# One Tanh of ScalarE moved behind copies in the projection, and one scaling on VectorE cut in two

## The chip, the cores and the metric

The kernel runs on one core of a Trainium2 chip. The metric is device time of one execution in microseconds (us); lower is better. A core has five engines that each work through their own list of instructions in order: TensorE (PE: matmul, with PEld for its weight loads), VectorE (DVE), ScalarE (ACT), GpSimd (POOL) and SyncE (SP, which here only issues transfers). They meet through semaphores: an instruction that needs another engine's result waits at the head of its engine's list, and all that is listed behind it waits too.

## The reference

`x` has 2048 tokens of 1024 features. It is normalised, and the normalised `xn` goes through two branches whose results are added to `x`:

```python
x = A_x
xn = _layernorm(x, axis=-1)
# branch A: a diagonal complex recurrence over the tokens
dt = jnp.exp(log_dt); Lam = Lambda_re + 1j * Lambda_im
Lam_bar = jnp.exp(dt * Lam)
B_bar = ((Lam_bar - 1.0) / Lam)[:, None] * Bmat
Bu = jnp.einsum("bld,pd->blp", x + 0j, B_bar)            # projection in (x is xn here)
h = Lam_bar[None, :] * h + Bu[:, t, :]                   # for every token t
y = 2.0 * jnp.einsum("blp,dp->bld", hseq, Cmat).real + x * Dskip
# branch B: a dense layer with mish
h = jnp.einsum("bsd,df->bsf", x, w1) + b1
sp = jnp.log1p(jnp.exp(-jnp.abs(h))) + jnp.where(h > 0, h, 0)
act = h * jnp.tanh(sp)
return jnp.einsum("bsf,fd->bsd", act, w2)
```

There are 1024 complex states, 3584 hidden features, and the output is bfloat16.

## The kernel before

The tokens are worked in four blocks of 512 (`blk` 0 to 3). A block has these stages, in the order in which TensorE goes through them:

1. First dense product (`first_tile`, line 777): 28 tiles `f` of 128 hidden features, 8 matmuls each, into PSUM bank `f % 8`. In blocks 1 to 3 ScalarE moves the first 7 tiles to `hb` with the bias (line 787), VectorE the others (line 790). Seven tiles are a group; when one is full, `mish` puts three activations on ScalarE over the whole group (128 x 3584): Exp (line 755), Ln of 1 + that (756), Tanh (757). `mish_mul` (762) is the product with `hb` on VectorE. Exp and Tanh need no table load between them, Ln needs one before it and Tanh one after it.
2. Projection into the states. Block 0 does it plainly (`project_in`). From block 1 on (`FAST = 1`) `project_fast` does it with seven products of half-size blocks in place of eight, for four pairs of state tiles a, b, c, d (`pr` 0 to 3). The order is the string `ORDER`: `c5` is product 5 of pair c (8 matmuls of 256 columns, line 834) and what takes its result away (`evacuate`); `r2` is the rotation of state tile 2 on VectorE (800 to 805); `u7` is a start on the second dense product for output unit 7 (6 matmuls, line 960); `m2` and `m3` are `mish_mul` of groups 2 and 3. A pair has three PSUM banks X, Y, Z; c has banks 4, 5, 6, and d has 0, 1, 2. Products 1, 6, 7 and 4 accumulate in X one after the other, and after products 1, 5 and 6 a copy of the partial sums is kept (a snapshot, `snaps`). Pairs a and b are copied by VectorE (849), pairs c and d by ScalarE (851): six copies a block. VectorE joins snapshots with other banks (859). The next product in bank X waits until the snapshot before it has been read out. There are four snapshot slots; a slot is free when its join has run. Product 4 goes from X to `hT` by a cast: on VectorE for a and b (876), on ScalarE for c and d (878).
3. Second dense product (`tail`, line 960, operands `ring` and `act`), then the recurrence's output projection (line 960, `ring` or in block 0 `CT`, and `hT`) into the same eight banks, one for each of the eight units of output. Meanwhile VectorE runs the rotations that are left, `mish_mul` of groups 2 and 3, the next block's normalisation and the recurrence (925 to 935).
4. `finish` (1027): VectorE adds banks and `x`, four times a block, two banks each. ScalarE issues the stores (1019).

Between block 0 and block 1 there is work that is done once: the rows of B and C are given scales by powers of two. `rows_C` writes a scaled C to DRAM (ScalarE, 1117, and its transfers, 1119). `scale_B(pr)` multiplies the two state tiles of a pair by a row, in two VectorE instructions, one for the real part (`ci` 0) and one for the imaginary part (`ci` 1), 128 x 2048 each (line 1126). `sums_B` (1137, 1138) then forms the sums that the seven products need. `scale_B(0)` is listed ahead of the four `finish` of block 0; `scale_B(1)` to `scale_B(3)` follow in `side(f)` of block 1, after tiles f = 0, 1 and 2. `rows_spread(1)` (1110) waits for a row that GpSimd's queue fetches (1103, 1105).

The lists are made in program order; nothing sorts them afterwards. So the place of a call is the place in its engine's list.

Of the kernel before, what the change touches and what calls it, by code (L numbers as in the profile page):

```python
# [163 lines left out]
def build_kernel(nc, A_x, A_Lambda_re, A_Lambda_im, A_B_re, A_B_im, A_C_re, A_C_im,  # L164
# [10 lines left out]
    NF = F // P  # L175
    GF = 7
# [4 lines left out]
    FAST = 1  # L181
# [7 lines left out]
    def sb(name, shape, dtype):  # L189
        return nc.alloc_sbuf_tensor(name, shape, dtype)  # L190
# [12 lines left out]
    act = sb("act", [P, NF, TB], bf16)  # L203
# [46 lines left out]
    def c(n):  # L250
        return cs[:, CN.index(n), :]
# [260 lines left out]
    def ln_skip(blk, q):  # L512

        i = blk % 2
        m = mt[:, q % 2, :, :].rearrange("p a t -> p (a t)")
        vop(lambda e: e.tensor_tensor(m, xn[:, q, :], dsk[:], op=ALU.mult),  # L516
            reads=[b_xn[q], b_dsk], writes=[b_m[q % 2]])
        vop(lambda e: e.tensor_tensor(xx[:, i, q, :], xx[:, i, q, :], m, op=ALU.add),
            reads=[b_xx[i][q], b_m[q % 2]], writes=[b_xx[i][q]])
# [7 lines left out]
    def b1(f):  # L527
        return par[:, 3 * NJ + f:3 * NJ + f + 1]
# [43 lines left out]
    def w1_tile(base, f, k):  # L572

        s = (base + 2 * (f // 4) + k // (NK // 2)) % NRING
        wt = ring[:, s, :].rearrange("p (k f) -> p k f", k=NK // 2)
        return s, wt[:, k % (NK // 2), (f % 4) * P:(f % 4 + 1) * P]
# [10 lines left out]
    def first_rest(f):  # L587

        for k in range(NK):
            s, w = w1_tile(0, f, k)  # L590
            PE.mm(lambda e, k=k, w=w: e.matmul(ps[:, f, 2 * P:4 * P], lhsT=w, rhs=xnT[:, k, 2 * P:4 * P],
                                               start=k == 0, stop=k == NK - 1),
                  reads=[b_ring[s]] + b_xnT[2:], writes=[b_ps[f]], first=k == 0, last=k == NK - 1)
# [155 lines left out]
               s_CT, writes=b_CT + b_early)  # L749


    def mish(g):
        hs = hb[:, (g % 2) * GF:(g % 2) * GF + GF, :]
        a = act[:, g * GF:(g + 1) * GF, :]
        aop(lambda e: e.activation(a, hs, AF.Exp), reads=[b_hb[g % 2]], writes=[b_act[g]])  # L755
        aop(lambda e: e.activation(a, a, AF.Ln, bias=1.0), reads=[b_act[g]], writes=[b_act[g]])  # L756
        aop(lambda e: e.activation(a, a, AF.Tanh), reads=[b_act[g]], writes=[b_act[g]])  # L757

    def mish_mul(g):
        hs = hb[:, (g % 2) * GF:(g % 2) * GF + GF, :]  # L760
        a = act[:, g * GF:(g + 1) * GF, :]
        vop(lambda e: e.tensor_tensor(a, a, hs, op=ALU.mult), reads=[b_act[g], b_hb[g % 2]], writes=[b_act[g]])  # L762
# [3 lines left out]
    def item_done():  # L766
        n_item[0] += 1
        ring_load()

    def first_tile(blk, f):  # L770
        bank, hs = f % 8, f % (2 * GF)
        raw = blk == 0 and f < NR
        if raw:
            first_rest(f)
        for k in range(0 if raw else NK):
            s, w = w1_tile(n_item[0], f % 4, k)
            PE.mm(lambda e, k=k, w=w: e.matmul(ps[:, bank, :], lhsT=w, rhs=xnT[:, k, :],  # L777
                                               start=k == 0, stop=k == NK - 1),
                  reads=[b_ring[s]] + b_xnT, writes=[b_ps[bank]], first=k == 0, last=k == NK - 1)
        if f % 4 == 3:  # L780
            item_done()
            item_done()
        if f % GF == 0 and f >= 2 * GF:
            mish_mul(f // GF - 2)
        ts = slice(2 * P if raw else 0, 4 * P)
        if blk and f < GF:
            aop(lambda e: e.activation(hb[:, hs, :], ps[:, bank, :], AF.Identity, bias=b1(f)),  # L787
                reads=[b_ps[bank], b_par], writes=[b_hbf[hs]])
        else:
            vop(lambda e: e.tensor_scalar(hb[:, hs, ts], ps[:, bank, ts], b1(f), None, op0=ALU.add),  # L790
                reads=[b_ps[bank], b_par], writes=[b_hbf[hs]])
        if f % GF == GF - 1:
            mish(f // GF)

    def banks_of(j):
        return 2 * ((j + 2) % 4)
# [41 lines left out]
    def evacuate(pr, n, keep):  # L838
# [34 lines left out]
        if n == 4:  # L873
# [3 lines left out]
            else:  # L877
                aop(lambda e: e.copy(dst, bank(X)), reads=[b_ps[X]], writes=b_hT[1][j0:j0 + 2])

    ORDER = ("a2 a1 b2 b1 a5 b5 a6 b6 a3 b3 a7 b7 c2 d2 a4 b4 c5 c1 r0 d5 d1 r1 c6 c3 d6 d3 "  # L880
             "c7 d7 u7 c4 r2 u5 d4 u6 u4 r3 r4 r5 r6 r7 m2 m3")

    def project_fast(open_unit):
        keep = {}
        for o in ORDER.split():
            kind, n = o[0], int(o[1])
            if kind == "r":
                rotate_in(n)
            elif kind == "u":
                open_unit(n)  # L890
            elif kind == "m":
                mish_mul(n)
            else:
                product("abcd".index(kind), n)
                evacuate("abcd".index(kind), n, keep)
# [213 lines left out]
    def rows_spread(h):  # L1109
        vop(lambda e: e.tensor_copy(srow[:, TB * h:TB * (h + 1)].rearrange("p (j q) -> p j q", q=P),  # L1110
                                    srow0[:, TB * h:TB * (h + 1)].rearrange("p (q j) -> p j q", q=P)),
            reads=[b_actf[26 + h]], writes=[b_actf[24 + h]])
# [5 lines left out]
            reads=[b_CT[j], b_si[j // 4]], writes=b_t)  # L1118
        AC.dma(lambda e: e.dma_start(ctd[j], t), s_ctd[j], reads=b_t, writes=[b_ctd[j]])

    def scale_B(pr):
        js = slice(2 * pr, 2 * pr + 2)
        b_B = b_BT[js]
        row = srow[:, 2 * P * pr:2 * P * (pr + 1)].rearrange("p (j q) -> p j q", j=2)
        for ci in range(2):
            vop(lambda e, ci=ci: e.tensor_tensor(  # L1126
                BT[:, ci, js, :, :], BT[:, ci, js, :, :], row.unsqueeze(2).to_broadcast([P, 2, NK, P]), op=ALU.mult),
                reads=b_B + [b_actf[24 + pr // 2]], writes=b_B)
# [25 lines left out]
    for blk in range(NB):  # L1154
        def side(f):
            if blk:
                if f in (8, 10, 12, 15):
                    ln_skip(blk, (8, 10, 12, 15).index(f))
                    if blk >= FAST:
                        sums_x((8, 10, 12, 15).index(f))  # L1160
                if blk == FAST:
                    if f == 1:
                        rows_spread(1)
                    if f < 3:
                        scale_B(f + 1)
                    if f in (3, 4, 17, 19):
                        sums_B((3, 4, 17, 19).index(f))
                return
            if f == 13:
                for j in range(NJ):  # L1170
                    table(j)
            if f in (5, 6, 7, 8):
                coefficients(f - 5)
            if f in (8, 9, 11, 12):
                ln_skip(0, (8, 9, 11, 12).index(f))
            if f in (14, 16, 18, 20):
                ln_stats_only(1, (f - 14) // 2)
            if f < 24 and f % 3 == 2:
                transpose_B(f // 3)
            if f >= 26:  # L1180
                transpose_C(f - 26)

        for f in range(NF):
            first_tile(blk, f)
            side(f)
        out_stage = tail(blk)
        open_unit = next(out_stage)
        if blk >= FAST:
            project_fast(open_unit)
        else:  # L1190
            project_in(blk)
        if 0 < blk < NB - 1:
            for q in range(NQ):
                ln_stats_only(blk + 1, q)
            ln_rsqrt()
            for q in range(NQ):
                ln_scale(blk + 1, q)
        if blk:
            next(out_stage)
        for j in range(NJ):  # L1200
            if blk == 0 and j == NJ - 1:
                rows_scale(0)
            recur(blk, j)
            if blk:
                continue
            if j == 0:
                mish_mul(3)
                ln_root()
                for q in range(NQ):
                    ln_scale(1, q)  # L1210
                next(out_stage)
                for i in range(NHS):
                    rows_load(i)
            scale_C(j)
            for i in {4: (0, 1, 2), 5: (3, 4, 5, 6), 6: (7, 8, 9, 10), 7: range(11, 16)}.get(j, ()):
                rows_size(i)
        if blk + 1 < NB:
            carry()
        if blk == FAST - 1:
            rows_scale(1)  # L1220
            vop(lambda e: e.tensor_tensor(qi[:], qi[:], c("ss").unsqueeze(1).to_broadcast([P, 2, NJ]), op=ALU.mult),
                reads=[b_qi] + b_ss, writes=[b_qi])
            rows_spread(0)
            scale_B(0)
            for j in range(NJ):
                rows_C(j)
        for _ in out_stage:
            pass
        if blk == FAST - 1:
            snaps_ready()  # L1230
# [36 lines left out]
```

## Time and profile before

| what | us |
|---|---|
| median of three runs | 615.79 (615.63 to 615.86) |
| the profiled execution's own time | 614.92 |
| its span, first to last instruction | 613.7 |
| TensorE busy in the span | 607.1 |
| VectorE busy | 491.1 |
| ScalarE busy | 306.5 |
| GpSimd busy | 95.3 |

The span is what the trace shows; 1.2 us of the execution's own time lie around it. The mean clock that was granted to TensorE is 1.000. The stages of the four blocks are found in the trace by their line numbers: the first dense product of block 1 begins at 162.02 us, of block 2 at 313.82 us. In the timeline's rows, a matmul group's length takes in the time until its last result is written, so a group that follows without a gap begins about 0.17 us before the end of the one ahead of it.

### The profile page before, as it was taken

How to read it: one execution, taken by the hardware profiler on the slowest of the kernel's cores; microseconds unless marked ns; L12 is line 12 of the kernel's file. 1: busy time of each engine (PE TensorE's matmuls, PEld its weight loads, DVE VectorE, ACT ScalarE, POOL GpSimd, SP SyncE). 2: the span in 40 equal slices, each digit the busy share in tenths (PEclk: the TensorE clock that was granted, in tenths of full speed). 3: DMA queues.
4: the chain of work that ended last, by engine and by line, in shares of the span. 5: the costliest groups of instructions: out<-in, count | busy, mean ns of one | idle time of the engine just before them, and what ended most of it. 6: DMA issues, size and time to landing. Idle time of an engine off the chain costs nothing.

```text
span 613.7 us, 8271 instructions
## 1 busy us (share of the span) xinstructions
PE 607.1 (99%) x3247; PEld 316.4 (52%) x3247; DVE 491.1 (80%) x780; ACT 306.5 (50%) x246; POOL 95.3 (16%) x89
## 2 busy tenths in 40 slices
PE   9999999999999989999999999999999999999998
PEld 8644444444444576444444468544444447844444
DVE  6989999999998949999724866999951776799923
ACT  4589998389879892000018997000003999400000
POOL 2899200221034000000013300000000510000000
PEclk9999999999999999999999999999999999999999
DMA  9999984991695400476565540049446443016411
GB/s 234 298 261 310 218 138 136 326 314 51 243 320 173 160 14 1 169 167 222 162 223 178 180 138 1 2 177 272 163 139 210 137 152 124 2 39 235 172 69 69
DMA packets 103969, 101.23 MB, mean 165 GB/s; under 512 B 51898, under 2 KB 81210, under 8 KB 103930
## 3 DMA queue, kind: packets, MB, share of 16 engines
q1 hardware_dynamic: 97840, 84.75, 47.5%
q0 software_dynamic: 2400, 7.61, 3.8%
q10 hardware_dynamic: 3690, 8.34, 3.5%
q8 instruction: 26, 0.43, 0.3%
q14 instruction: 13, 0.11, 0.0%
HBM read 80.23 MB, written 8.39 MB: 144 GB/s over the span
## 4 chain that ended last, share of the span: by engine, by line
PE 61%; DVE 19%; ACT 15%; issue 3%; DMA 1%; POOL 1%; SPq 0%; ACTq 0%; DVEq 0%; POOLq 0%
PE ps L960 37%; PE ps L777 16%; PE ps L834 8%; ACT act L756 3%; ACT act L755 3%; ACT act L757 3%; DVE hT L925 3%; DVE hb L790 2%; DVE CT L736 2%; DVE CT L733 2%; DVE mt L930 1%; ACT L756 1%; DVE BT L1126 1%; DMA xx<-in_A_x_dram 1%; ACT tab L671 1%
## 5 line engine op out<-in xcount | busy, mean ns | idle before, releaser
L960 PE MATMUL ps<-ring,act 128*128 128x512 bf16 x896 | 195.0, 379 | 0.0
L777 PE MATMUL ps<-xnT,ring 128*128 128x512 bf16 x840 | 181.9, 379 | 0.4 <-DVE xx L1027 0.4
L960 PEld LDWEIGHTS ps<-ring,act 128*128 128x128 bf16 x896 | 87.6, 98 | 103.8
L777 PEld LDWEIGHTS ps<-xnT,ring 128*128 128x128 bf16 x840 | 82.2, 98 | 99.5 <-issue 0.9
L790 DVE TENSOR_SCALAR hb<-ps,par 128x512 bf16<-128x512 f32 (+1 forms) x91 | 63.1, 723 | 44.0 <-PE ps L777 43.1
L787 ACT ACTIVATE hb<-ps,par 128x512 bf16<-128x512 f32 x21 | 13.8, 692 | 165.0 <-PE ps L777 165.0
L960 PE MATMUL ps<-ring,hT 128*128 128x512 bf16 x378 | 82.1, 379 | 0.0
L960 PEld LDWEIGHTS ps<-ring,hT 128*128 128x128 bf16 x378 | 37.0, 98 | 44.6
L925 DVE TENSOR_TENSOR_SCAN hT<-cs,qi,hT 128x512 bf16<-128x512 f32 x48 | 58.9, 1268 | 0.0
L755 ACT ACTIVATE act<-hb 128x3584 bf16<-128x3584 bf16 x16 | 50.9, 3183 | 7.3 <-DVE hb L790 7.3
L756 ACT ACTIVATE act<-act 128x3584 bf16<-128x3584 bf16 x16 | 51.0, 3190 | 0.2
L757 ACT ACTIVATE act<-act 128x3584 bf16<-128x3584 bf16 x16 | 51.0, 3190 | 0.2
L930 DVE TENSOR_TENSOR mt<-hT,tab 128x1024 bf16<-128x1024 bf16 x64 | 41.4, 688 | 1.1
L762 DVE TENSOR_TENSOR act<-act,hb 128x3584 bf16<-128x3584 bf16 x16 | 35.2, 2218 | 3.6 <-ACT act L757 3.6
L1143 POOL TENSOR_TENSOR TT<-xnT 128x1024 f16<-128x1024 bf16 x6 | 15.5, 2584 | 143.7 <-DVE mt L516 143.7
L1027 DVE TENSOR_TENSOR xx<-ps,xx 128x1024 bf16<-128x1024 f32 (+1 forms) x16 | 18.8, 1189 | 21.1 <-PE ps L960 21.0
L859 DVE TENSOR_TENSOR hT<-ps,snaps 128x512 f16<-128x512 f32 x36 | 24.0, 688 | 10.8 <-ACT snaps L851 8.4
L800 DVE TENSOR_TENSOR mt<-hT,tab 128x1024 bf16<-128x1024 f16 x48 | 31.0, 686 | 0.5
L339 POOL DMA_DIRECT2D xx<-in_A_x_dram x12 | 6.7, 557 | 136.8 <-DVE xx L1027 114.7
L902 PE MATMUL ps<-xnT,BT 128*128 128x512 bf16 x128 | 27.8, 379 | 0.0
L960 PE MATMUL ps<-CT,hT 128*128 128x512 bf16 x128 | 27.8, 379 | 0.0
L834 PE MATMUL ps<-TT,SS 128*128 128x256 f16 x192 | 23.4, 273 | 2.3 <-ACT snaps L851 2.3
(144 smaller groups left out, 651.8 us busy)
## 6 DMA issues: line engine op xcount, KB each, us to landing
ring<-in_B_w_dram SPq DMA_DIRECT2D x112, 512.0 KB, 4.7
ring<-ctd SPq DMA_DIRECT2D x24, 512.0 KB, 3.3
ctd<-act ACTq DMA_DIRECT2D x8, 512.0 KB, 4.2
out_dram<-xx ACTq DMA_DIRECT2D x15, 256.0 KB, 4.4
xx<-in_A_x_dram POOLq DMA_DIRECT2D x12, 256.0 KB, 6.0
act<-in_A_B_re_dram POOLq DMA_DIRECT2D x8, 256.0 KB, 5.0
act<-in_A_B_im_dram POOLq DMA_DIRECT2D x8, 256.0 KB, 5.1
xx<-in_A_x_dram SPq DMA_DIRECT2D x3, 256.0 KB, 5.5
```

Source lines behind the costliest of these rows:

```text
L755: aop(lambda e: e.activation(a, hs, AF.Exp), reads=[b_hb[g % 2]], writes=[b_act[g]])
L756: aop(lambda e: e.activation(a, a, AF.Ln, bias=1.0), reads=[b_act[g]], writes=[b_act[g]])
L757: aop(lambda e: e.activation(a, a, AF.Tanh), reads=[b_act[g]], writes=[b_act[g]])
L762: vop(lambda e: e.tensor_tensor(a, a, hs, op=ALU.mult), reads=[b_act[g], b_hb[g % 2]], writes=[b_act[g]])
L777: PE.mm(lambda e, k=k, w=w: e.matmul(ps[:, bank, :], lhsT=w, rhs=xnT[:, k, :], start=k == 0, stop=k == NK - 1), reads=[b_ring[s]] + b_xnT, ...
L790: vop(lambda e: e.tensor_scalar(hb[:, hs, ts], ps[:, bank, ts], b1(f), None, op0=ALU.add), reads=[b_ps[bank], b_par], writes=[b_hbf[hs]])
L800: vop(lambda e, s=s: e.tensor_tensor(mt[:, s, :, :], hT16[:, :, j, :], tab[:, s, j, :].unsqueeze(1).to_broadcast([P, 2, TB]), op=ALU.mult) ...
L834: PE.mm(lambda e, w=w, x=x, o=o, begin=begin, end=end: e.matmul(ps[:, bank, o:o + TH], lhsT=w, rhs=x, start=opens and begin, stop=end, ski ...
L902: PE.mm(lambda e, j=j, ci=ci, k=k, bank=bank: e.matmul(ps[:, bank + ci, :], lhsT=BT[:, ci, j, k, :], rhs=xnT[:, k, :], start=k == 0, stop= ...
L925: vop(lambda e, ci=ci, init=init: e.tensor_tensor_scan(out=hT[:, ci, j, :], data0=cj("r", j).to_broadcast([P, TB]), data1=hT[:, ci, j, :], ...
L930: vop(lambda e, s=s: e.tensor_tensor(mt[:, s, :, :], hT[:, :, j, :], tab[:, s, j, :].unsqueeze(1).to_broadcast([P, 2, TB]), op=ALU.mult), ...
L960: PE.mm(lambda e: e.matmul(ps[:, u, :], lhsT=lhsT, rhs=rhs, start=st_, stop=last), reads=reads, writes=[b_ps[u]], first=st_, last=last, te ...
```

## The change

The last group's Tanh of blocks 1 to 3 is taken out of `mish` and put into `ORDER` as `t3`, after product d6 and ahead of d3. On ScalarE's list, where Tanh and its table load stood ahead of the six snapshot copies of pairs c and d, they now stand behind them and ahead of the two casts of c4 and d4. The other mish groups, and block 0, are as they were. The second edit lists the `ci` 1 half of `scale_B(0)` behind the four `finish` of block 0, at the start of what `side(0)` of block 1 puts on VectorE; the `ci` 0 half stays ahead of them. No instruction is added or left out.

```diff
-    def mish(g):
+    def mish(g, hold=False):
...
         aop(lambda e: e.activation(a, a, AF.Ln, bias=1.0), reads=[b_act[g]], writes=[b_act[g]])
+        if not hold:
+            mish_tanh(g)
+
+    def mish_tanh(g):
+        a = act[:, g * GF:(g + 1) * GF, :]
         aop(lambda e: e.activation(a, a, AF.Tanh), reads=[b_act[g]], writes=[b_act[g]])
...
         if f % GF == GF - 1:
-            mish(f // GF)
+            mish(f // GF, hold=blk >= FAST and f == NF - 1)
...
-    ORDER = ("a2 a1 b2 b1 a5 b5 a6 b6 a3 b3 a7 b7 c2 d2 a4 b4 c5 c1 r0 d5 d1 r1 c6 c3 d6 d3 "
+    ORDER = ("a2 a1 b2 b1 a5 b5 a6 b6 a3 b3 a7 b7 c2 d2 a4 b4 c5 c1 r0 d5 d1 r1 c6 c3 d6 t3 d3 "
              "c7 d7 u7 c4 r2 u5 d4 u6 u4 r3 r4 r5 r6 r7 m2 m3")
...
+            elif kind == "t":
+                mish_tanh(n)
...
-    def scale_B(pr):
+    def scale_B(pr, cis=(0, 1)):
...
-        for ci in range(2):
+        for ci in cis:
...
                 if blk == FAST:
                     if f == 1:
                         rows_spread(1)
+                    if f == 0:
+                        scale_B(0, (1,))
                     if f < 3:
                         scale_B(f + 1)
...
-            scale_B(0)
+            scale_B(0, (0,))
```

## The prediction

> **What bounds the kernel now.** I read the busy shares first: TensorE is busy for 607.1 of a 613.7 us span, so a change that adds no work and takes none away can only give what TensorE waits. The list of TensorE's waits, then, says how much that is and where:
>
> ```profile
> PE ps L834 <- ACT snaps L851: 2.3, 1, 2.3
> ...
> PE ps L834 <- DVE hT L859: 0.4, 1, 0.4
> PE ps L777 <- DVE xx L1027: 0.4, 1, 0.4
> ```
>
> Columns: who waits, for whom, us in total, times, longest. Each wait occurs once, while the same lines run in three blocks. The busy time by stage shows which block (projection of blocks 1, 2, 3):
>
> ```profile
> 210.36:240.44 30.08, 27.39 (x237) 22.92 (x236) 20.88 (x36) 22.50 (x15) 0.00 (x0) 1.00 0.11 36
> ...
> 362.17:389.21 27.04, 27.04 (x237) 23.09 (x236) 20.61 (x35) 17.48 (x13) 0.00 (x0) 1.00 0.11 40
> ...
> 510.94:537.99 27.05, 27.05 (x238) 23.10 (x237) 20.61 (x35) 17.49 (x13) 0.00 (x0) 1.00 0.11 40
> ```
>
> After the length come TensorE, its weight loads, VectorE, ScalarE. The projection fills TensorE in blocks 2 and 3 and leaves it 2.7 us idle in block 1, where ScalarE carries 5 us more. The timeline there tells why (start, length, engine, idle before and its releaser):
>
> ```profile
> 224.34 1.04 PE L834 MATMUL ps<-TT,SS 128*128 128x256 f16 x8
> ...
> 224.77 1.28 ACT L757 ACT_TABLE_LOAD   x1
> ...
> 226.07 3.19 ACT L757 ACTIVATE act<-act 128x3584 bf16<-128x3584 bf16 x1
> ...
> 229.16 2.03 ACT L851 COPY snaps<-ps 128x512 f32<-128x512 f32 x4
> 230.25 0.69 DVE L859 TENSOR_TENSOR hT<-ps,snaps 128x512 f16<-128x512 f32 x1 [5.02 <-ACT snaps L851]
> ...
> 230.27 1.05 PE L834 MATMUL ps<-TT,SS 128*128 128x256 f16 x8 [2.28 <-ACT snaps L851]
> ```
>
> The first row is c5, done at 225.38. Its snapshot stands behind Tanh and is taken at 229.16; c6, which must not overwrite the bank before c1's copy, waits. ScalarE is late here since block 1's activations began late, after the eight scaled copies of C (L1117, the last at 167.38) and four store issues. In block 2 the same Tanh is long over and ScalarE waits for TensorE:
>
> ```profile
> 372.42 3.19 ACT L757 ACTIVATE act<-act 128x3584 bf16<-128x3584 bf16 x1
> ...
> 377.22 0.59 ACT L851 COPY snaps<-ps 128x512 f32<-128x512 f32 x1 [1.61 <-PE ps L834]
> ...
> 382.46 0.59 ACT L851 COPY snaps<-ps 128x512 f32<-128x512 f32 x1 [1.16 <-PE ps L834]
> ...
> 387.25 0.59 ACT L878 CAST hT<-ps 128x512 f16<-128x512 f32 x1 [4.20 <-PE ps L834]
> ```
>
> The third wait is at the start of block 1:
>
> ```profile
> 158.25 2.49 DVE L1126 TENSOR_TENSOR BT<-BT,act 128x2048 bf16<-128x2048 bf16 x2
> ...
> 160.65 4.61 DVE L1027 TENSOR_TENSOR xx<-ps,xx 128x1024 bf16<-128x1024 f32 x4
> ...
> 162.02 4.26 PE L777 MATMUL ps<-xnT,ring 128*128 128x512 bf16 x19 [0.39 <-DVE xx L1027]
> ```
>
> Two scalings stand ahead of the first addition, which frees banks 0 and 1 for block 1's first tiles.
>
> **Step 1, the halved scaling.** One BT instruction of 1.24 us leaves the place ahead of the additions. The first addition needs the first quarter of block 0's last state tile. The 128 matmuls of that output projection begin at 133.84 and take 27.62 us to the next start where nothing waits (block 2's: 286.20 to 313.82), so they would end their issue at 161.46; the quarter is 12 matmuls of 27.62/128 = 0.216 us earlier, 158.87, plus 0.17 to write: 159.04. The remaining half scaling ends at 158.25 + 1.24 = 159.5. So the addition (1.2 us) ends at 160.7, ahead of 161.46, and TensorE need not wait. It now starts at 162.02: gain 0.56 us. (The view says 0.39; it counts from the modelled end, 0.17 after the issue.) The following additions need banks that TensorE uses from tile 2 on, 3.5 us later.
>
> The half that is moved costs nothing behind them: VectorE's total up to there is the same, its chain from 158.25 to 188.4 has no gap, and then it idles 2.23 us until Tanh of group 0 ends at 190.6. That idle is the cover. Queued behind the moved half are the scalings of pair 1, `rows_spread(1)`, which starts at 167.57 as before, and the sums; tile 0's eviction is ScalarE's. If GpSimd's fetch of the row (issued at 163.77 before) came later, VectorE could lose 2.1 us before Exp of group 1 on ScalarE, at 190.49, felt it (the last `hb` it needs ends at 188.4). The stores are issued at 169.78, when ScalarE is done with C, so additions that end 1.2 us earlier (164.1) start no transfer sooner.
>
> **Step 2, Tanh behind the snapshots.** The built order on the engines differs in the places named and nowhere else; there is one table load ahead of Tanh as before, none at the copies or casts. In block 1, Ln ends at 221.56 + 3.19 = 224.75. Between 172.92 and there ScalarE and VectorE hand each other the work (Exp of group 2 waits for `hb` at 204.98, `mish_mul` for Tanh), neither waits for TensorE (L787 at 172.92 is noted as waiting for it, but ScalarE's queue issues stores until 172.87), so an earlier TensorE doesn't move 224.75. With TensorE 0.56 earlier, the projection starts at 209.80, a shift of -152.37 against block 2's 362.17. The first c5 copy can then start at 377.22 - 152.37 = 224.85, 0.10 after Ln. Copies take 0.59 and products come every 0.87, so a late ScalarE catches up 0.28 with each. VectorE is also just in time: its last `hb` ends at 211.69, a1's copy is due at 364.12 - 152.37 = 211.75. From there block 1 is block 2 shifted: the long dense stretch begins at 389.21 - 152.37 = 236.84, not 240.44.
>
> What becomes late is Tanh. It starts after d6's copy; block 2's times: 382.46 + 0.59 = 383.05, load 1.28, gap 0.01, Tanh 3.19, end 387.54. The c4 cast, due at 387.25, comes 0.29 late, d4's (389.41) not at all. Behind c4's cast are the rotation r4, which VectorE reaches at 390.54, and unit u4 in the same bank, for which TensorE has yet to do u5, d4 and u6 (1.30 + 0.87 + 1.30 from c4's end, about 387.2: 390.7). The cast ends at 388.1, so 2.4 us stay. Tanh's own reader, m3, is behind r7; in block 1 it ran after 250.46, against an end of 235.2. Price in blocks 2 and 3: nothing; without that cover each us past 2.4 would hold VectorE a us. Copies under Ln's table rather than Tanh's are not in the trace. L787's activation takes 0.69 in block 2 (after Tanh) and 4.16 for 7 in block 1 (after Sqrt's table), so the table doesn't matter there: I take 0.59 and no extra load, with 0 to 1.28 us (a load) as bounds. The high end, paid once, is 1.28 less ScalarE's catching up: c1's copy would start at 224.75 + 1.28 + 0.59 = 226.6, 0.9 after it is due. VectorE's last join before c4 would come that much later, against some 0.3 to spare (four joins from 383.90 at some 0.6 each, the third read by c4 at 386.17): TensorE loses 0.6.
>
> [...]
>
> **Sum.** Step 1: 0.56. Step 2: block 1 from its first tile to the long stretch is now 240.44 - 162.02 = 78.42 us, block 2's is 389.21 - 313.82 = 75.39; gain 3.03. Together 3.59 us. Check from the waits: 2.28 + 0.41 + 0.39 and three times 0.17 is 3.59. After 240.6 the chain of waits is TensorE alone to its last matmuls, so the gain is kept to the end: span 613.70 - 3.59 = 610.11, the profiled execution 614.92 - 3.59 = 611.33, the median 615.79 - 3.59 = 612.2.
>
> **Rivals.**
> (a) Only part comes, since two margins in block 1 are thin (0.10 on ScalarE, 0.06 on VectorE). If the activations end 1 us later, c1's copy is late by 1.0 - 0.10 - 0.28 = 0.6 and TensorE waits 0.3 at c4; a load at the copies gives 0.6; if step 1 is held by something unseen, 0.56. One or two of these: 612.5 to 613.4. For it: the margins. Against it: both chains are fixed by durations that repeat to 0.01 us between blocks.
> (b) The gain is handed back: TensorE, 3.6 us earlier in block 1's second dense product, waits for weights or states there. Time 615.8. For it: other engines' work is the same. Against it: VectorE's rotations move with the copies, the weights with TensorE's releases, and blocks 2 and 3 run the same lines in that spacing with no wait.
> (c) Slower: Tanh holds the two casts in all three blocks. Place: L878 behind L757. Price: each us that c4's cast is past 390.5 delays r4 and u4. It decides when Tanh ends over 2.4 us later than worked out; to be slower by 1.2 us the three blocks must eat 3.59 + 1.23, 1.6 each, so Tanh 4.0 us later: 612.2 + 3 x 1.6 = 617.0. For it: six waits on TensorE stand right before it, and d6's copy needs a free slot, for which it waited 1.71 in block 1. Against it: that wait would give Tanh's end 233.65 + 0.59 + 4.48 = 238.7, at most 0.25 past the old cast.
>
> **How the numbers follow.** Forecast 0.86 (611.8 to 612.5: 3.59 is all that TensorE waits there, and runs differ by 0.2); (a) 0.08; (b) 0.03; (c) 0.03. A measurement here tells 0.2% (1.23 us) from no change. (a) is still faster by more than that: faster 0.94, same 0.03, slower 0.03. The range takes in most of (a): 611.8 to 613.1.
>
> **What would show it.** Right: TensorE's list of waits without L851, L859 and L1027; block 1's projection 27.05 long; six copies in block 1 that wait for TensorE, a Tanh after them ending about 0.3 after c4 is due. Wrong: a wait of TensorE for L859 or L878 in blocks 1 to 3, a table load between Ln and the copies, or a new wait between 237 and 310.

## The result, and the profile after

| | before | changed |
|---|---|---|
| median of four runs, us | 615.82 (615.63 to 615.86) | 611.58 (611.08 to 612.24) |
| profiled execution, own time and span, us | 614.92, 613.7 | 611.78, 610.5 |
| TensorE busy, us | 607.1 | 602.9 |

The ratio is 0.9932, 95% interval 0.9915 to 0.995: faster, by 4.24 us in the medians where 3.59 was forecast. The forecast time, 612.2, is 0.6 too high, and the range (611.8 to 613.1) does not hold the result. The two profiled executions differ by 3.14 us.

TensorE's waits in the changed kernel, in the list of waits (from `mish` on, line numbers are now higher by 5 to 7):

```profile
PE ps L582 <- DMA ring<-in_B_w_dram: 1.9, 1, 1.9
PE ps L544 <- DVE filler L386: 1.0, 1, 1.0
```

All three waits of the forecast are gone. What is left lies in the first 8 us: a wait for an operand of zeros, and one for the first weights. The chain that ended last agrees; before, its first line read 61% PE, 19% DVE and 15% ACT:

```profile
PE 98%; DMA 1%; issue 0%; SPq 0%; DVE 0%
```

The projections of blocks 1, 2 and 3 in the busy time by stage (length, then TensorE, its weight loads, VectorE, ScalarE, GpSimd, granted clock):

```profile
210.28:237.32 27.04, 26.99 (x237) 23.08 (x236) 21.56 (x37) 23.16 (x15) 0.00 (x0) 1.00 0.13 40
359.05:386.09 27.04, 26.99 (x236) 23.09 (x236) 20.61 (x35) 17.36 (x13) 0.00 (x0) 1.00 0.11 40
507.82:534.86 27.04, 26.99 (x236) 23.10 (x236) 20.61 (x35) 17.37 (x13) 0.00 (x0) 1.00 0.11 40
```

Block 1 has become like the others: 27.04 where it was 30.08. The timeline in block 1 shows how:

```profile
221.85 3.19 ACT L756 ACTIVATE act<-act 128x3584 bf16<-128x3584 bf16 x1
...
225.32 0.58 ACT L856 COPY snaps<-ps 128x512 f32<-128x512 f32 x1 [0.28 <-PE ps L839]
226.19 0.58 ACT L856 COPY snaps<-ps 128x512 f32<-128x512 f32 x1 [0.29 <-PE ps L839]
...
230.56 0.58 ACT L856 COPY snaps<-ps 128x512 f32<-128x512 f32 x1 [1.16 <-PE ps L839]
231.16 1.28 ACT L762 ACT_TABLE_LOAD   x1
...
232.46 3.19 ACT L762 ACTIVATE act<-act 128x3584 bf16<-128x3584 bf16 x1
...
235.15 1.46 PE L967 MATMUL ps<-ring,act 128*128 128x512 bf16 x6
235.56 0.57 ACT L883 CAST hT<-ps 128x512 f16<-128x512 f32 x1
```

Ln ends at 225.04 and ScalarE is then the one that waits, 0.28 us for c5. There is no load between Ln and the copies. Tanh's table load comes behind the sixth copy, and c4's cast at 235.56 starts 0.41 behind the matmuls that follow c4 (235.15). In block 2 of the kernel before, where nothing held it, that distance was 0.20 (387.05 and 387.25), so the cast is 0.21 late. At the start of block 1:

```profile
158.69 1.22 DVE L1133 TENSOR_TENSOR BT<-BT,act 128x2048 bf16<-128x2048 bf16 x1
...
159.83 4.61 DVE L1034 TENSOR_TENSOR xx<-ps,xx 128x1024 bf16<-128x1024 f32 x4
...
161.93 4.26 PE L782 MATMUL ps<-xnT,ring 128*128 128x512 bf16 x18
```

One scaling stands ahead of the additions, and TensorE's first tile has no wait.

### The profile page after: what moved, and what is told of

Same layout as the page of the kernel before. It is cut to its first block, busy times and chain, and to the rows that moved or that the text cites. A ratio compares the mean times of both kernels' runs of the same rounds, so it can differ in the third digit from the quotient of the medians.

```text
span 610.5 us, 8221 instructions
## 1 busy us (share of the span) xinstructions
PE 602.9 (99%) x3197; PEld 315.7 (52%) x3247; DVE 491.1 (80%) x780; ACT 306.6 (50%) x246; POOL 94.7 (16%) x89
## 4 chain that ended last, share of the span: by engine, by line
PE 98%; DMA 1%; issue 0%; SPq 0%; DVE 0%
PE ps L967 49%; PE ps L782 30%; PE ps L839 12%; PE ps L909 5%; PE ps L582 1%; PE ps L591 1%; DMA ring<-in_B_w_dram 1%; PE ps L992 0%; PE ps L434 0%; SPq L343 0%; PE ps L469 0%; DVE xx L1057 0%; SPq L339 0%; PE ps L617 0%
## 5 line engine op out<-in xcount | busy, mean ns | idle before, releaser
L839 PE MATMUL ps<-TT,BT 128*128 128x256 f16 x192 | 23.4, 273 | 0.0
```

Of the source, the lines that this page charges most:

```text
L839: PE.mm(lambda e, w=w, x=x, o=o, begin=begin, end=end: e.matmul(ps[:, bank, o:o + TH], lhsT=w, rhs=x, start=opens and begin, stop=end, ski ...
```

## The experiments

The question was where the 0.65 us came from that the medians gained beyond the sum. The runs of one set share a chip, and each set has runs of the kernel before beside it; "mean clock" is the clock granted to TensorE, averaged over an execution.

**The kernel before, once more** (unchanged).

> The kernel before, unchanged, to see what its executions do that the one profiled execution (614.92 us, against a median of 615.8) did not. Theory 1 (one size of stall): TensorE's gaps before block 2 are the same 3.6 us in every execution, the median 615.8 holds, and the 0.65 us that the changed kernel was better than forecast is chance. Theory 2 (two chains): before, ScalarE and VectorE set the end up to block 1's projection, and in most executions they come later than in the one profiled, so TensorE waits longer for the copies there: this profile, where its time is about 615.8, shows the wait of line 834 for line 851 some 0.5 to 1.0 us above 2.28, with the later blocks' spacing unchanged.

Median 615.9 of ten; this profiled execution took 616.19, 1.27 more than the first one. Its TensorE around c6 in block 1, in the timeline, and the granted clock in stretches of 2 us (length, TensorE busy, clock):

```profile
230.64 1.89 PE L834 MATMUL ps<-TT,SS 128*128 128x256 f16 x8 [2.89 <-ACT snaps L851]
232.32 1.74 PE L834 MATMUL ps<-xnT,SS 128*128 128x256 bf16 x8
233.90 1.04 PE L834 MATMUL ps<-TT,SS 128*128 128x256 f16 x8
```

```profile
228.00:230.00 2.00, 0.00 (x0) 1.00 0.00 0
230.00:232.00 2.00, 1.36 (x7) 0.58 0.00 0
232.00:234.00 2.00, 2.00 (x12) 0.56 0.00 0
234.00:236.00 2.00, 2.00 (x21) 1.00 0.00 0
```

The wait is 0.61 longer, as theory 2 has it, but the rows show something that neither theory had: after it, sixteen matmuls of 256 columns take 3.26 us from start to start instead of 1.75. The clock granted to TensorE fell to half (0.50) at 230.34 us, while TensorE waited, and stayed there until 233.75. In the first profiled execution the wait was 2.28 us and c6 ran at full clock (1.00 from 226 to 236 us). So that execution was without a part of the price that this one paid. From here on this is theory C: the wait costs its length, and often a stretch at half the clock behind it.

**Each edit alone.** Only the Tanh moved (the first scaling undivided ahead of the additions), and only the scaling halved (`mish` and `ORDER` as before). The main lines of the second:

```diff
-    def scale_B(pr):
+    def scale_B(pr, cis=(0, 1)):
...
+                    if f == 0:
+                        scale_B(0, (1,))
...
-            scale_B(0)
+            scale_B(0, (0,))
```

> Only the Tanh is moved; both halves of the first scaling stay ahead of the additions. By the working of the forecast: the gap in the projection goes (3.03 us by the profiled execution), the one at block 1's start (0.56) stays: 612.8 from the median, ratio 0.995. Theory 2: the gap in the projection is larger in most executions, so 612.0 to 612.3, 0.5 above the changed kernel.

> Only the first scaling is halved; Tanh stays ahead of the copies. If gains add up, 0.56 us less than before: 615.2. If ScalarE's copies set the projection's end, as both theories have it, TensorE comes 0.56 us earlier to the same late copy and waits 0.56 us longer there: 615.8, nothing gained, and the profile shows the wait of line 834 for line 851 at about 2.9 us instead of 2.3 in an execution like the one profiled.

Tanh alone: 612.8 (four runs, 611.8 to 613.56) beside 616.46 for the kernel before on that chip. Halving alone: 615.44, ratio 0.9988 (0.9974 to 1.0002), no gain that can be told. Six of its ten executions were at full clock, and their median, 615.0, is that of the kernel before at full clock (614.98, in the table further down). The list of waits of its profiled execution (616.89) says why:

```profile
PE ps L834 <- ACT snaps L851: 3.5, 1, 3.5
```

TensorE came to block 1 without its wait for the addition and waited the longer for the copies, and the matmuls behind that wait ran at half clock again (0.50 from 232 to 234 us). So the two gains do not simply add up: the second shows only where the first has been made. The first trace of Tanh alone had a wait of 1.65 us for weights in block 0 and none for the addition: TensorE came late to block 1 anyway. It was run again:

> Only the Tanh moved, once more, since the first trace of it had a wait for a transfer of weights in block 0 (1.65 us) that made TensorE late and so hid the scaling. By the forecast's sum TensorE waits some 0.4 us for the addition at block 1's start wherever no transfer has held it before, and the time is up to 0.56 us above the changed kernel's 611.5: 611.6 to 612.2, all at the full clock. If halving the scaling brings more than that, 612.5 and more again.

612.36 (six runs, three of them 611.48 to 611.55, the others 613.18 to 614.97). All were expected at full clock; the slowest, which is not the one profiled, had a mean clock of 0.997. The wait for the addition is back in the profiled one, of 611.55 us:

```profile
PE ps L782 <- DVE xx L1034: 0.4, 1, 0.4
```

0.36 us in the timeline, so 0.53 with the 0.17 of a broken stream: the forecast's 0.56 holds in the trace. In the times of so few runs it can't be told from the spread.

**The changed kernel again**, on the chip of the next three:

> The changed kernel again, beside the variants of this set on one chip. TensorE waits nowhere between its first weights and the end, so the time is that of its start plus a constant: 611 to 612.3 as before, and a granted clock of 1.00 in every stage. Against a kernel before of about 616.4 the ratio is 0.992 to 0.993, a gain of 4.3 to 5.0 us, more than the 3.59 of the forecast.

611.54 (611.27 to 612.02) beside 615.98: ratio 0.9915 (0.9896 to 0.9934). All eight executions of the changed kernel have a mean clock of 1.000. The profiled one (612.02) had a wait of 0.66 us for weights in block 0, which was not expected behind the first weights; there was none from block 1 on.

**The wait filled with useless work**: 36 matmuls of zeros ahead of c6, so that TensorE is not idle there. The main lines:

```diff
+            if blk == FAST and o == "c6":
+                keep_busy(36)
...
```

> The kernel before with 36 matmuls of zeros (128 columns, some 2.0 us) listed just ahead of c6 in block 1, where TensorE waits; they add no result and ScalarE's order is untouched. Theory C (clock): after a wait of 2.9 us and more the next matmuls run at half the clock for some 3 us, which costs 1.5 us; with the wait filled to under 1 us that goes: 614.7 to 615.0, 1.3 to 1.6 below the kernel before, and clock 1.00 in the projection of block 1. Theory 2 without the clock (only the length of the wait counts): the late copy is as late as ever, 616.4, no gain, or slower by what the fillers are too long.

615.61 (614.67 to 618.94) beside 615.98: ratio 0.9996 (0.9977 to 1.0014). By the medians this does not decide: the spread of both is too wide. Nine of the ten executions had a mean clock of 1.000, against five of 19 of the kernel before on that chip. The profiled one was the tenth, and its half clock came elsewhere, after a wait of 2.02 us for weights in block 0 (0.50 from 56 to 58 us); in block 1 it was 1.00.

**More work on TensorE**, in tile 20 of block 0, in both kernels:

```diff
-        for k in range(0 if raw else NK):
+        for k in [-1] * (5 if blk == 0 and f == 20 else 0) + list(range(0 if raw else NK)):
+            again, k = k < 0, max(k, 0)
...
```

> The kernel before with five matmuls more: tile 20 of block 0 runs its first one five times again (5 x 0.216 = 1.08 us of TensorE). ScalarE and VectorE have slack there. If the wait for the copies takes it all up and nothing else: no change, 616.4. Theory C: the wait shrinks from 2.3 to 2.9 down to 1.2 to 1.8, the clock stays, and the kernel with more work is faster by up to 1.5: 614.7 to 615.2. Theory 1 (fixed sum): no change.

> The changed kernel with the same five matmuls. TensorE is its bound from the first weights on, so all of the 1.08 us reaches the end: 612.6 to 613.0, against some 611.6 without. If something else still sets the end anywhere, less.

Before: 615.92, no change, so the waits do take up the added work; but half of the executions (five of ten) still had the lower clock, a mean of 0.997, and the hoped-for gain of up to 1.5 is not there. In the profiled one (614.85) the wait for the copies was 2.04 us, where 1.2 to 1.8 was expected, since the wait for the addition is gone from its list and had taken a part; the clock stayed at 1.00. Changed: 612.8 against 611.54, all of the 1.08 us and a little more by medians. The profiled one, the slowest of the four (613.7), also waited 1.32 us in block 0 (at 51.3) for VectorE to empty a bank; from block 1 on TensorE waits for nothing in it.

**More work on ScalarE**: half of the last scaled copy of C is done twice, on the chain that ends in block 1's copies. The added instruction was expected to cost 1.04 us and takes 1.15 in the traces. In the kernel before, in the same with the wait filled (54 zero matmuls), and in the changed one:

```diff
+        if j == NJ - 1:
+            aop(lambda e: e.activation(t[:, 0:1024], CT[:, j, 0, :], AF.Copy, scale=cj("si", j)),
+                reads=[b_CT[j], b_si[j // 4]], writes=b_t)
```

> The kernel before with half of the last scaled copy of C run twice on ScalarE, 1.04 us more on the chain that ends in block 1's copies. If that chain sets the end: the wait of line 834 for line 851 grows to 3.3 to 3.9 us, the matmuls after it run at half the clock, and the execution's own time lies 390.9 to 391.1 us after the end of block 1's last Ln, as in the two earlier traces with a halved clock there, against 390.2 in the three without. Median about 617. If TensorE's own work sets the end, no change.

> The same with 54 matmuls of zeros (3.0 us) ahead of c6 in block 1. The copies are as late as in the run beside it. Theory C (the clock is a part of the price of the wait): clock 1.00 in the projection, the time 390.2 us after the end of the last Ln, and 0.8 to 0.9 us less than without the fillers in the profiled executions, measured from that Ln. Theory 2 without the clock: 390.9 to 391.1 again.

> The changed kernel with the same 1.04 us more on ScalarE. By the forecast's margins (0.1 to 0.3 us until c5's copy is late, 0.28 caught up with the next product, 0.3 on VectorE) c1's copy is 0.4 to 0.6 late and TensorE waits 0.1 to 0.4 us at c4, where the kernel before loses all of the 1.04: time 611.6 to 612.2. If ScalarE still sets the end: 612.6.

Before with it: 619.12 (617.33 to 620.82), ratio 1.0054 (1.0029 to 1.0079), and none of the five executions at full clock (means of 0.994 and 0.997). Filled: 616.99 (615.8 to 618.05), ratio 1.0021 (1.0009 to 1.0034), all ten at full clock. The fillers add 3 us of useless matmuls and take 2.1 us off. First the one without, then the one with fillers, in the timeline and in the busy time of 232 to 234 us (length, TensorE busy, clock):

```profile
223.71 3.19 ACT L756 ACTIVATE act<-act 128x3584 bf16<-128x3584 bf16 x1
...
232.42 1.89 PE L834 MATMUL ps<-TT,SS 128*128 128x256 f16 x8 [3.96 <-ACT snaps L851]
234.10 1.92 PE L834 MATMUL ps<-xnT,SS 128*128 128x256 bf16 x8
235.81 1.91 PE L834 MATMUL ps<-TT,SS 128*128 128x256 f16 x8
```

```profile
232.00:234.00 2.00, 1.58 (x8) 0.50 0.00 0
```

```profile
223.48 3.19 ACT L756 ACTIVATE act<-act 128x3584 bf16<-128x3584 bf16 x1
...
228.07 3.18 PE L544 MATMUL ps<-filler 128*128 128x128 bf16 x54
232.19 1.05 PE L834 MATMUL ps<-TT,SS 128*128 128x256 f16 x8 [0.94 <-ACT snaps L851]
233.08 1.04 PE L834 MATMUL ps<-xnT,SS 128*128 128x256 bf16 x8
```

```profile
232.00:234.00 2.00, 1.81 (x17) 1.00 0.00 0
```

c6 starts 5.52 us after the end of Ln in both (226.90 and 226.67), so the copies are equally late, and the same eight matmuls take 1.89 in one and 1.05 in the other. This decides for theory C: only the clock differs, 0.50 in one and 1.00 in the other. The size expected for it (0.8 to 0.9) was too small, since with the wait of 3.96 us the clock stayed down for 6.8 us (231.05 to 237.88), twice the 3.4 us measured with the waits of 2.89 and 3.49.

In the changed kernel the added work costs 0.3 by medians, 611.86 (611.1 to 612.33) against 611.54 on another chip. In the profiled execution it costs more: block 1's projection takes 27.60 us (209.03 to 236.63), 0.56 above the 27.04. TensorE breaks off twice. Product b2 starts at 211.12, 0.34 later than in an unbroken stream (16 matmuls of 256 columns from 209.03 take 1.75); the list of waits has it behind VectorE, which is late with its last move to `hb`:

```profile
PE ps L839 <- DVE hb L795: 0.2, 1, 0.2
```

Then ScalarE's copies come late and catch up, and c4 starts 0.19 us after TensorE is ready for it (u7 begins at 232.09, six matmuls of 0.216 end their issue at 233.39):

```profile
225.36 1.54 ACT L856 COPY snaps<-ps 128x512 f32<-128x512 f32 x3
...
233.58 1.05 PE L839 MATMUL ps<-TT,BT 128*128 128x256 f16 x8
```

**The first weights in two halves**, on the changed kernel, since TensorE sets its time from there on. The main lines:

```diff
+        if i == 0:
+            for h in range(2):
+                SP.dma(lambda e, h=h: e.dma_start(dst[:, 2 * h:2 * h + 2, :], src[:, 2 * h:2 * h + 2, :]),
+                       DmaSem(nc, "d_first%d" % h), writes=[b_ring[s].parts[h]])
+            return
...
-    for f in range(4):
-        first_raw(f, 0, NK // 2)
+    for k in (0, 2):
+        for f in range(4):
+            first_raw(f, k, k + 2)
```

> The changed kernel with its first load of weights as two transfers of 256 KB, and the first 16 matmuls ordered by half, so that eight of them need the first half alone. TensorE now sets the end from its first weights on; where it waits for them (1.87 us in the changed kernel's first profile, 0 to 0.4 in others) up to 0.9 us of work comes ahead: median 611.1 to 611.6. If the second half lands later than the whole did, or the weights are rarely last, no difference: 611.5.

No gain, where 611.1 to 611.6 was expected: 613.54, in two groups, four executions at 611.05 to 611.62 and five at 613.54 to 614.25, all at full clock. The profiled one is of the lower group and shows no wait above 0.5 us behind the start. What the upper group waits for is open. No version that was run has a lower median than the changed kernel.

## Why the prediction missed

**What the mechanism was right about.** Step 1: the addition's wait is gone, and it is there again when the scaling is undivided (0.53 against 0.56 worked out). Step 2: block 1's projection takes 27.04 us (forecast 27.05). c4's cast comes 0.21 late (0.29). Nothing behind it waits. From the first matmul of block 0's projection to the start of the last ones it was 610.07 - 57.86 = 552.21 us and is 606.95 - 58.33 = 548.62: 3.59 us, the sum as worked out. The forecast for the profiled execution itself was 611.33; measured 611.78, and the 0.45 between them is its start, where TensorE had waited 1.87 us for weights against 0.30 and reached line 591 at 15.94 instead of 15.48. All signs that were named for a right forecast are there.

**The step that failed** is the last of the sum: "the median 615.79 - 3.59 = 612.2", with the range's floor, "3.59 is all that TensorE waits there". It took one execution's waits for the whole price in every execution. The lengths of the waits were right for that execution, but a term is missing from the sum, and so stood at nothing: the time that TensorE loses at half clock behind the wait (0.75 to 2.06 us in the three traces that show it there, below). That execution had no such stretch; 56 of the 78 below have a lowered mean clock. The spread under the floor was too small as well: "runs differ by 0.2" rests on three runs, and the 78 below lie up to 4.2 us apart. The executions of the unchanged kernel on four chips, sorted by mean granted clock:

```
kernel before              executions   median us   lowest    highest
mean clock 1.000                   22      614.98   614.38     616.67
mean clock 0.997 or less           56      616.24   615.48     618.62
changed kernel, 1.000               8      611.54   611.08     612.24
```

By the measured stretches, 3.4 us at half clock lower the mean over 615 us by 0.003 (3.4 x 0.5 / 615). The three profiled executions of 0.997 (once more, scaling halved, filled) each have one such stretch, the one of 0.994 (ScalarE longer) one of 6.8 us. So 0.997 is taken for one stretch of 3.4 us; where it lay is known only for the profiled executions. The first profiled execution (614.92) was of the rarer kind. 614.98 - 3.59 = 611.39 is within 0.15 of the changed kernel, so the sum holds among executions at full clock. From the other kind the gain is 616.24 - 611.54 = 4.7: the 3.59, the clock (0.75 and 0.91 in the two traces with one stretch behind the wait, below), and 0.2 to 0.4 that these do not cover. In the result, 615.82 lies 0.84 above 614.98 and 611.58 lies 0.19 above 611.39, which makes 3.59 + 0.84 - 0.19 = 4.24. The clock of the first timed runs (615.63 to 615.86) was not recorded; that they were of the second kind is argued from their times: of the 11 executions in the table between 615.6 and 615.9, ten have the lowered clock.

The clock's own price can be read from the traces of the unchanged order, where the copies set the end. The time that lies behind the end of block 1's last Ln (execution time less that moment):

```
                          Ln ends   time     behind   wait    clock after it
first profile              224.75   614.92   390.17   2.28    1.00
tile 20 longer             224.70   614.85   390.15   2.04    1.00
filled                     228.79   618.94   390.15   0.35    1.00
ScalarE longer, filled     226.67   616.83   390.16   0.94    1.00
once more                  225.12   616.19   391.07   2.89    half
scaling halved             225.98   616.89   390.91   3.49    half
ScalarE longer             226.90   619.12   392.22   3.96    half
```

(The wait is that of c6 for the copies; where it is filled, what is left of it.) In all seven c6 starts 5.52 us after that moment, so it is the copies that release it, and a longer wait means only that TensorE was there earlier. The four traces with a clock of 1.00 after the wait agree within 0.02 us, whatever the wait. The halved ones lie 0.91, 0.75 and 2.06 above 390.16. The rest of the spread before is the moment at which Ln ends, 224.70 to 228.79. The latest, 228.79, comes after 2.02 us of waiting for weights in block 0 and a stretch at half clock there; what moves the others apart, other than the work that was added, was not followed up.

**The rivals.** (a) did not come, but its margins are as thin as it says: with more work on ScalarE, Ln ended 1.65 us later against line 591 (225.45 - 14.70, in place of 225.04 - 15.94); TensorE lost 0.19 at c4, where (a) had some 0.3 for 1 us, and 0.34 at b2, where VectorE was late, a place that (a) did not price. (b) did not: there is no wait behind 237 us. (c) did not: c4's cast is 0.21 late in block 1, with 2.4 to spare. None of them was a larger gain, and that is the side on which it went: the forecast priced the wait at its length only.

## What to carry to other kernels

A wait of TensorE as long as this one (2.02 to 3.96 us in six traces here, four of them with half clock after it) is priced at its length and, as a likely case with its own bounds, a stretch at half clock behind it (0.75 to 2.06 us in the three traces where it lay in block 1), even where the one trace at hand shows full clock. Before a sum from one profiled execution is carried to a median, look whether the execution's own time lies within the runs: here it was 0.7 below the lowest of three, a sign that the typical run paid something that the trace did not show. Two waits of one engine in a row need not be two gains: here, removing the first alone only lengthened the second (3.49 us in its trace, against 2.28 and 2.89).

## What the runs showed of the hardware

In four traces the granted clock fell to 0.50, three times for 3.4 us and once for 6.8. The edges are worked out from the mean clock of windows of 0.5 to 2 us. It lasted from 230.34 to 233.75 in the kernel run once more, from 230.84 to 234.24 with the scaling halved, and from 231.05 to 237.88 with ScalarE longer. It began 2.6, 2.8 and 2.6 us after TensorE had stopped. In the filled run it lasted from 55.04 to 58.44 in block 0 and began 0.4 us after TensorE had resumed from its wait for weights (54.64). Waits of 2.02, 2.89, 3.49 and 3.96 us were followed by half clock, waits of 2.04 and 2.28 were not. What decides between 2.02 and 2.28 was not tried.
